# Forming the low part of each weight piece on GpSimd instead of VectorE

## The chip, the core and the metric

The kernel runs on one core of a Trainium2 chip. The metric is the device time of one execution in microseconds, the median over runs; a profile of one execution is beside it. The engines are TensorE (PE, matrix products; PEld is its loading of weights), VectorE (DVE), ScalarE (ACT), GpSimd (POOL) and SyncE (SP, which issues the DMAs). Each engine works through its own list of instructions in order, and waits at an instruction until the ones that it depends on have reported.

## The reference

```python
def _attn_ref(q, k, v):                       # 2 x 8 heads, 768 positions, 64 wide
    block, window = (32, 16)
    k_sum = k.reshape(B, H, nb, block, D).max(axis=3)
    v_sum = v.reshape(B, H, nb, block, D).mean(axis=3)
    scores_l = scale * np.matmul(q, k.transpose(0, 1, 3, 2))    # masked to |i - j| < window
    scores_s = scale * np.einsum('bhsd,bhnd->bhsn', q, k_sum) + np.log(block)
    a = softmax over both together
    return np.matmul(a, v_all)                # v and v_sum

x = attention output, 1536 tokens x 512
y = (x @ w_a) * (x @ w_b) @ w_out             # 512 -> 1536 -> 512
h = y @ w_in;  out = np.maximum(0.01 * h, h) @ w_out2   # 512 -> 2048 -> 512
```

q, k, v and the result are float32. The five dense weights arrive as float64, two 32-bit words for a number; the kernel builds a float32 value from both words.

## The kernel before

Attention is done in pairs of windows (transposes, scores, a softmax on ScalarE and VectorE, transposes of the weights, products with v), and writes x as two float32r tiles, a high part (rounded) and the low part that is left. Every dense product is then three matmuls: high by high, high by low, low by high (`mm3`, L580). One such matmul has 512 columns.

The weights come in 68 pieces of 128 x 512 numbers (`a` and `b`, f = 0 to 11; `o`, 12; `i` and `p`, 16 each). A piece is staged by a DMA of 512 KB and converted in seven steps: `low` (L337, VectorE, and L341, ScalarE), `clamp` (L345), `shift` (L350), `join` (L356), `add` (L362), all on VectorE, `high` (L367: ScalarE rounds to float32r) and `rest_of` (L370: the float32 value less that rounded part, the low part of the piece). The steps stand in a list, `bg`, from which a few are taken at a time between the products (`interleave`, `tick`). A piece lies in one of 14 early buffers, later of 8 more, until its last use. The tile `wc` has two buffers: a piece's L341 needs that the subtraction (L370) of the piece two before is done.

The dense part has nine passes, `units`: (s, c) with s a third of the hidden size (four f) and c one of three chunks of 512 tokens. A pass runs four pairs of an a product and a b product (12 matmuls each), and after each pair forms g = a * b and splits it: ScalarE copies a (L608), VectorE multiplies (L612), ScalarE rounds (L600), VectorE subtracts (L601, tile gs). Then the pass's y products run (48 matmuls in four groups of 12, two groups at a time: the first three f of both, 18 matmuls, then the fourth f of both). The last gs of a pass is therefore first read by the 19th matmul of its y products. While s = 0 the attention of the next chunk runs between the products. The last stage (L787, L788, L601) does the same for h, with the o products one product behind.

The order of each engine's list is made by the framework's scheduler when the program is built, from times that it assumes for each instruction; it need not be the order of the code. GpSimd has, after some constants at the start, one kind of work: the copies of the block sums of v into the windows (`put_sums`, L191), 16 of them, the last at about 140 us. Attention's other steps on VectorE that are named below are L528 (scores, reads PSUM), L542 (weights times 1/sum, reads SBUF), L479 and L428 (reductions), L573 (low part of x, one operand in PSUM); L680 and L685 gather y from PSUM.

Of the kernel before, what the change touches and what calls it, by code (L numbers as in the profile page):

```python
# [21 lines left out]
def kernel(  # L22
# [12 lines left out]
    nc = tc.nc  # L35
# [269 lines left out]
    def stage():  # L305
        key = pieces[cnt["st"]]
        cnt["st"] += 1
        nm, f = key
        t = wst_p.tile([P, 1024], I32, tag="wst", name="wst")
        if nm in "op":  # L310
            src = {"o": w_o, "p": w_o2}[nm][P * f : P * (f + 1), :]
            nc.sync.dma_start(out=t, in_=src)
        else:
            src = {"a": w_a, "b": w_b, "i": w_i}[nm][:, 2 * P * f : 2 * P * (f + 1)]
            nc.sync.dma_start(
                out=t.rearrange("p (k f) -> p k f", k=KT),
                in_=src.rearrange("(k p) f -> p k f", p=P),
            )
        staged[key] = t

    def convert():

        i = cnt["conv"]
        key = pieces[i]
        while cnt["st"] < min(i + 4, len(pieces)):
            stage()
        cnt["conv"] += 1
        ww = staged.pop(key).rearrange("p (f two) -> p f two", two=2)
        lo_w, hi_w = ww[:, :, 0], ww[:, :, 1]
        home = "early" if room["early"] else "late"  # L330
        assert room[home], key
        room[home] -= 1
        t = {}

        def low():
            t["r"] = wcv_p.tile([P, 512], I32, tag="wr", name="wr", bufs=1)
            nc.vector.tensor_scalar(  # L337
                out=t["r"], in0=lo_w.bitcast(U32), scalar1=2.0**-29, scalar2=None, op0=ALU.mult
            )
            t["c"] = wcv_p.tile([P, 512], I32, tag="wc", name="wc")  # L340
            nc.scalar.activation(out=t["c"].bitcast(F32), in_=hi_w.bitcast(F32), func=AF.Abs)  # L341

        def clamp():
            c = t["c"].bitcast(F32)
            nc.vector.tensor_scalar(  # L345
                out=c, in0=c, scalar1=F_LO, scalar2=F_HI, op0=ALU.max, op1=ALU.min
            )

        def shift():
            nc.vector.tensor_scalar(  # L350
                out=t["c"], in0=t["c"], scalar1=3, scalar2=0x3FFFFFF8,
                op0=ALU.logical_shift_left, op1=ALU.bitwise_and,
            )

        def join():
            nc.vector.scalar_tensor_tensor(  # L356
                out=t["c"], in0=hi_w, scalar=-0x40000000, in1=t["c"],
                op0=ALU.bitwise_and, op1=ALU.bitwise_or,
            )

        def add():
            nc.vector.tensor_tensor(out=t["c"], in0=t["c"], in1=t["r"], op=ALU.add)  # L362

        def high():
            pool = wsp_p if home == "early" else late["wsp"]
            t["w"] = pool.tile([P, 2, 512], F32R, tag="wsp", name="wsp")
            nc.scalar.copy(out=t["w"][:, 0], in_=t["c"].bitcast(F32))  # L367

        def rest_of():
            nc.vector.tensor_tensor(  # L370
                out=t["w"][:, 1], in0=t["c"].bitcast(F32), in1=t["w"][:, 0].bitcast(F32),
                op=ALU.subtract,
            )
            w_of[key] = t["w"], home

        bg.extend([low, clamp, shift, join, add, high, rest_of])
# [454 lines left out]
```

## Time and profile before

| | us |
|---|---|
| median of 3 runs | 662.12 (661.54 to 662.96) |
| the profiled execution | 661.62 |
| its span, first to last instruction | 659.9 |
| TensorE busy | 635.6 |
| VectorE busy | 422.0 |
| ScalarE busy | 267.8 |
| GpSimd busy | 21.1 |

The span is that of one execution taken by the hardware profiler; 1.7 us of its time lie around it. Busy time is the time in which an engine has an instruction under way; matmuls overlap, and their ends are modelled. A wait is put down to the instruction that reported last before the waiting one began. The granted clock is the share of TensorE's full speed that the chip allowed in a stretch.

### The profile page before, as it was taken

The numbers are of one execution on the slowest core, as the hardware profiler recorded it, in microseconds if no ns is written. First come the engines' busy times: TensorE is split into PE (matmuls) and PEld (weight loads), VectorE is DVE, ScalarE is ACT, GpSimd is POOL, SyncE is SP. The second block draws the span as 40 slices with busy tenths as digits, with TensorE's granted clock in tenths as the row PEclk, the third lists the DMA queues.
The fourth block names the chain that finished last, engine by engine and source line by source line (L and its number), as shares of the span: only waits on it lengthen the run. The fifth ranks groups of instructions, "written<-read, shape, count | busy, mean of one in ns | idle before, by whom it ended". The sixth has DMA issues, their size and how long they took to land.

```text
span 659.9 us, 9321 instructions
## 1 busy us (share of the span) xinstructions
PE 635.6 (96%) x3448; PEld 518.4 (79%) x3448; DVE 422.0 (64%) x968; ACT 267.8 (41%) x607; POOL 21.1 (3%) x38
## 2 busy tenths in 40 slices
PE   5699799999999999999999999999999999999997
PEld 4567577777888888888888888888888888888886
DVE  5989999955999972699623779732279532422323
ACT  4677386653445421344222535322255322222221
POOL 3210020000000000000000000000000000000000
PEclk9899799999999999999999999999999999999999
DMA  9976543512334430143200232400014000100101
GB/s 239 258 174 162 148 107 109 151 26 65 125 130 133 156 96 1 64 125 121 74 1 0 67 93 77 147 1 1 0 51 141 1 0 1 64 1 1 64 1 64
DMA packets 72590, 53.43 MB, mean 81 GB/s; under 512 B 46176, under 2 KB 66656, under 8 KB 72544
## 3 DMA queue, kind: packets, MB, share of 16 engines
q1 hardware_dynamic: 72544, 52.84, 27.0%
q8 instruction: 27, 0.44, 0.3%
q14 instruction: 19, 0.16, 0.1%
HBM read 49.68 MB, written 3.15 MB: 80 GB/s over the span
## 4 chain that ended last, share of the span: by engine, by line
PE 89%; DVE 7%; ACT 2%; DMA 1%; issue 1%; SPq 0%; DVEq 0%; ACTq 0%
PE ps_t L580 38%; PE ps_c L580 19%; PE ps_a L580 14%; PE ps_b L580 13%; PE ps_t L515 2%; DVE pm L528 1%; PE ps_t L550 1%; PE ps_t L562 1%; ACT pm L532 1%; DVE v L428 1%; DVE pm L542 1%; DMA wst<-in_moe_w_b_dram 1%; DVE wc L356 1%; PE ps_t L497 1%; DVE wr L337 0%
## 5 line engine op out<-in xcount | busy, mean ns | idle before, releaser
L580 PE MATMUL ps_t<-x,wsp 128*128 128x512 f32 x336 | 78.6, 389 | 0.0
L580 PE MATMUL ps_c<-wsp,gs 128*128 128x512 f32 x288 | 75.8, 389 | 0.0
L580 PE MATMUL ps_t<-wsp,gs 128*128 128x512 f32 x288 | 74.7, 389 | 0.0
L580 PEld LDWEIGHTS ps_t<-x,wsp 128*128 128x128 f32 x336 | 63.1, 188 | 13.1
L580 PE MATMUL ps_t<-ys,wsp 128*128 128x512 f32 x288 | 71.9, 389 | 0.0
L580 PE MATMUL ps_a<-x,wsp 128*128 128x512 f32 x252 | 68.6, 410 | 3.0 <-DVE wsp L370 2.7
L341 ACT ACTIVATE wc<-wst 128x512 f32<-128x512 f32 x68 | 45.6, 673 | 55.3 <-DMA wst<-in_moe_w_out_dram 12.1
L580 PE MATMUL ps_b<-x,wsp 128*128 128x512 f32 x252 | 64.3, 394 | 0.5 <-DVE wsp L370 0.5
L580 PEld LDWEIGHTS ps_t<-ys,wsp 128*128 128x128 f32 x288 | 54.1, 188 | 11.2
L580 PEld LDWEIGHTS ps_c<-wsp,gs 128*128 128x128 f32 x288 | 54.0, 188 | 11.2
L580 PEld LDWEIGHTS ps_t<-wsp,gs 128*128 128x128 f32 x288 | 54.0, 188 | 11.2
L580 PE MATMUL ps_c<-gs,wsp 128*128 128x512 f32 x240 | 60.8, 394 | 0.0
L580 PEld LDWEIGHTS ps_a<-x,wsp 128*128 128x128 f32 x252 | 47.9, 194 | 14.2 <-DVE wsp L370 3.1
L788 DVE SCALAR_TENSOR_TENSOR h<-h,ps_t 128x512 f32<-128x512 f32 x24 | 16.5, 686 | 60.8 <-ACT h L787 60.8
L580 PEld LDWEIGHTS ps_b<-x,wsp 128*128 128x128 f32 x252 | 46.6, 188 | 10.6 <-DVE wsp L370 1.0
L370 DVE TENSOR_TENSOR wsp<-wc,wsp 128x512 fp32r<-128x512 f32 x68 | 47.2, 696 | 9.9 <-ACT wsp L367 9.8
L580 PEld LDWEIGHTS ps_c<-gs,wsp 128*128 128x128 f32 x240 | 44.4, 188 | 9.5 <-ACT x L572 0.2
L367 ACT CAST wsp<-wc 128x512 fp32r<-128x512 f32 x68 | 42.1, 622 | 19.6 <-DVE wc L362 13.8
L580 PE MATMUL ps_t<-gs,wsp 128*128 128x512 f32 x192 | 47.7, 390 | 0.0
L601 DVE TENSOR_TENSOR gs<-h,gs 128x512 fp32r<-128x512 f32 x48 | 33.1, 691 | 22.8 <-ACT gs L600 22.7
L362 DVE CUSTOM_DVE_ANT_0 wc<-wc,wr 128x1024 uint16<-128x1024 uint16 x68 | 46.6, 685 | 0.6
L356 DVE SCALAR_TENSOR_TENSOR wc<-wst,wc 128x512 int32<-128x512 int32 x68 | 46.7, 689 | 0.2
(86 smaller groups left out, 835.9 us busy)
## 6 DMA issues: line engine op xcount, KB each, us to landing
wst<-in_moe_w_out_dram SPq DMA_DIRECT2D x28, 512.0 KB, 3.3
wst<-in_moe_w_in_dram SPq DMA_DIRECT2D x16, 512.0 KB, 3.7
wst<-in_moe_w_a_dram SPq DMA_DIRECT2D x12, 512.0 KB, 3.6
wst<-in_moe_w_b_dram SPq DMA_DIRECT2D x12, 512.0 KB, 3.6
k<-in_k_dram SPq DMA_DIRECT2D x16, 192.0 KB, 3.5
vb<-in_v_dram SPq DMA_DIRECT2D x6, 512.0 KB, 5.3
out_dram<-acc SPq DMA_DIRECT2D x12, 256.0 KB, 2.1
q<-in_q_dram SPq DMA_DIRECT2D x16, 128.0 KB, 2.9
```

Source lines behind the costliest of these rows:

```text
L341: nc.scalar.activation(out=t["c"].bitcast(F32), in_=hi_w.bitcast(F32), func=AF.Abs)
L356: nc.vector.scalar_tensor_tensor(out=t["c"], in0=hi_w, scalar=-0x40000000, in1=t["c"], op0=ALU.bitwise_and, op1=ALU.bitwise_or,)
L362: nc.vector.tensor_tensor(out=t["c"], in0=t["c"], in1=t["r"], op=ALU.add)
L367: nc.scalar.copy(out=t["w"][:, 0], in_=t["c"].bitcast(F32))
L370: nc.vector.tensor_tensor(out=t["w"][:, 1], in0=t["c"].bitcast(F32), in1=t["w"][:, 0].bitcast(F32), op=ALU.subtract,)
L428: lambda i=i, d=d: nc.vector.tensor_reduce(out=v0[:, i, d : d + D // 2], in_=vb_tiles[i][:, :, d : d + D // 2].rearrange("p j d -> p d j") ...
L497: nc.tensor.transpose(ps[:, n * P : (n + 1) * P], q2[:, n].rearrange("p c d -> p (c d)"), ident)
L515: nc.tensor.matmul(out=ps[h, w, :], lhsT=qt[h, w * W : (w + 1) * W], rhs=kts[h, (g * G + w) * SC : (g * G + w) * SC + P], start=True, stop ...
L528: pace["after"] = nc.vector.tensor_tensor_reduce(out=pm[:, w, :], in0=ps[:, w, :], in1=m, scale=1.0, scalar=3.0e38, op0=ALU.add, op1=ALU.m ...
L580: nc.tensor.matmul(out=ps, lhsT=w(a), rhs=x(b), start=first and j == 0, stop=last and j == 2)
L601: nc.vector.tensor_tensor(out=t[:, 1], in0=src, in1=t[:, 0].bitcast(F32), op=ALU.subtract)
L788: nc.vector.scalar_tensor_tensor(out=h, in0=h, scalar=0.01, in1=ps, op0=ALU.mult, op1=ALU.max)
```

## The change

`rest_of` is issued on GpSimd instead of VectorE. Operands, types and tiles stay.

```diff
         def rest_of():
-            nc.vector.tensor_tensor(
+            nc.gpsimd.tensor_tensor(
                 out=t["w"][:, 1], in0=t["c"].bitcast(F32), in1=t["w"][:, 0].bitcast(F32),
                 op=ALU.subtract,
             )
```

The scheduler makes new lists from it. GpSimd, from its first copies on (vw_99 and vw_100 are the two tiles of windows of v; wsp is a piece's high and low part), before:

```order
L191 COPY vw_99<-vs 24x1024
L191 COPY vw_100<-vs 24x1024
L191 COPY vw_99<-vs 24x1024
L191 COPY vw_100<-vs 24x1024
L191 COPY vw_99<-vs 24x2x256 x2
L191 COPY vw_100<-vs 24x2x256 x2
L191 COPY vw_99<-vs 24x2x256 x2
```

And now:

```order
L191 COPY vw_99<-vs 24x1024
L191 COPY vw_100<-vs 24x1024
L191 COPY vw_99<-vs 24x1024
L370 TENSOR_TENSOR wsp<-wc,wsp 128x512 x2
L191 COPY vw_100<-vs 24x1024
L191 COPY vw_99<-vs 24x2x256 x2
L370 TENSOR_TENSOR wsp<-wc,wsp 128x512
L191 COPY vw_100<-vs 24x2x256
L370 TENSOR_TENSOR wsp<-wc,wsp 128x512
L191 COPY vw_100<-vs 24x2x256
L370 TENSOR_TENSOR wsp<-wc,wsp 128x512 x2
```

The subtractions stand between the copies; 14 come before the last copy, 54 behind it.

VectorE at the second piece, early in attention (wc and wr are the piece being converted, pm and nb the scores), before:

```order
L362 ISA wc<-wc,wr 128x1024
L542 TENSOR_TENSOR pm<-pm,sm 128x512
L486 COPY kts_94<-ks_98 128x12x24
L370 TENSOR_TENSOR wsp<-wc,wsp 128x512
L528 ISA pm,nb<-ps_t_509,negm_first 128x128
```

And now:

```order
L362 ISA wc<-wc,wr 128x1024
L542 TENSOR_TENSOR pm<-pm,sm 128x512
L486 COPY kts_94<-ks_98 128x12x24
L528 ISA pm,nb<-ps_t_509,negm_first 128x128
L528 ISA nb 128x1
```

L370 is gone from the list, and the scores follow directly.

VectorE at the end of the fourth pass (s = 1, c = 0), up to its last gs, before:

```order
L362 ISA wc<-wc,wr 128x1024
L345 TENSOR_SCALAR wc<-wc 128x512
L337 TENSOR_SCALAR wr<-wst 128x512
L350 TENSOR_SCALAR wc<-wc 128x512
L370 TENSOR_TENSOR wsp<-wc,wsp 128x512
L356 SCALAR_TENSOR_TENSOR wc<-wst,wc 128x512
L612 TENSOR_TENSOR g<-ps_t_2614,g 128x512
L362 ISA wc<-wc,wr 128x1024
L345 TENSOR_SCALAR wc<-wc 128x512
L337 TENSOR_SCALAR wr<-wst 128x512
L601 TENSOR_TENSOR gs<-g,gs 128x512
```

And now:

```order
L350 TENSOR_SCALAR wc<-wc 128x512
L356 SCALAR_TENSOR_TENSOR wc<-wst,wc 128x512
L362 ISA wc<-wc,wr 128x1024
L345 TENSOR_SCALAR wc<-wc 128x512
L337 TENSOR_SCALAR wr<-wst 128x512
L350 TENSOR_SCALAR wc<-wc 128x512
L612 TENSOR_TENSOR g<-ps_t_2614,g 128x512
L356 SCALAR_TENSOR_TENSOR wc<-wst,wc 128x512
L362 ISA wc<-wc,wr 128x1024
L601 TENSOR_TENSOR gs<-g,gs 128x512
```

More conversion steps stand in front of the same L612 and L601. From the last L601 of the third pass to this one the list held nine L362, eight L356 and eight L370 before; now it holds ten L362 and ten L356.

## Rows read from the trace of the kernel before

**Rows 1.** The page: busy us and share of each engine; VectorE in 40 slices.
```profile
PE 635.6 (96%) x3448; PEld 518.4 (79%) x3448; DVE 422.0 (64%) x968; ACT 267.8 (41%) x607; POOL 21.1 (3%) x38
...
DVE  5989999955999972699623779732279532422323
```

**Rows 2.** Windows: start:end us, length, busy of each engine, granted clock, DMA.
```profile
16.50:99.00 82.50, 69.37 (x707) 54.11 (x708) 76.78 (x251) 57.45 (x195) 11.76 (x13) 0.94 0.65 170
...
69.20:75.80 6.60, 5.06 (x16) 3.67 (x18) 6.60 (x12) 1.07 (x2) 0.00 (x0) 0.50 0.73 197
99.00:165.00 66.00, 66.00 (x508) 50.43 (x507) 48.16 (x154) 37.23 (x109) 4.08 (x3) 1.00 0.30 88
165.00:231.00 66.00, 66.00 (x293) 54.62 (x292) 62.61 (x126) 31.97 (x54) 0.00 (x0) 1.00 0.41 136
```

**Rows 3.** Waits: engine, what waited <- for what: total us, times, longest.
```profile
PE ps_a L580 <- DVE wsp L370: 2.7, 1, 2.7
...
PE ps_t L562 <- POOL vw L191: 1.0, 1, 1.0
...
ACT wc L341 <- DMA wst<-in_moe_w_out_dram: 12.1, 8, 2.3
```

**Rows 4.** Groups by line, and L191 alone: duration ns min/median/max.
```profile
L370 DVE TENSOR_TENSOR wsp<-wc,wsp 128x512 fp32r<-128x512 f32 x68 | 47.2, 696 | 9.9 <-ACT wsp L367 9.8
...
L191 POOL COPY vw<-vs x16: 607/1081/1507, 20.5 to 140.0; 24x1024 f32<-24x1024 f32 x8, 24x512 f32<-24x512 f32 x8
```

**Rows 5.** Windows of L370 alone: start:end, length, VectorE busy.
```profile
16.50:99.00 82.50, 6.26 (x8) 0.94 0.65 170
```

**Rows 6.** Timeline of VectorE beside two copies: start us, duration us, instruction.
```profile
105.13 0.69 DVE L362 CUSTOM_DVE_ANT_0 wc<-wc,wr 128x1024 uint16<-128x1024 uint16 x1
105.74 1.26 DVE L345 TENSOR_SCALAR wc<-wc 128x512 f32<-128x512 f32 x1
...
123.87 0.69 DVE L573 TENSOR_TENSOR x<-ps_t,x 128x512 fp32r<-128x512 f32 x1
124.48 0.61 DVE L350 TENSOR_SCALAR wc<-wc 128x512 int32<-128x512 int32 x1
```

**Rows 7.** Timeline of GpSimd: copies of 1024 elements; the first meets no wait.
```profile
94.39 1.10 POOL L191 COPY vw<-vs 24x1024 f32<-24x1024 f32 x1 [6.36 <-PE ps_t L562]
105.32 1.40 POOL L191 COPY vw<-vs 24x1024 f32<-24x1024 f32 x1 [9.84 <-PE ps_t L562]
123.35 1.46 POOL L191 COPY vw<-vs 24x1024 f32<-24x1024 f32 x1 [16.64 <-PE ps_t L562]
```

**Rows 8.** Timeline of VectorE at the end of the third pass.
```profile
189.60 0.42 DVE L350 TENSOR_SCALAR wc<-wc 128x512 int32<-128x512 int32 x1
189.94 0.68 DVE L370 TENSOR_TENSOR wsp<-wc,wsp 128x512 fp32r<-128x512 f32 x1
190.54 0.68 DVE L356 SCALAR_TENSOR_TENSOR wc<-wst,wc 128x512 int32<-128x512 int32 x1
191.14 0.68 DVE L601 TENSOR_TENSOR gs<-g,gs 128x512 fp32r<-128x512 f32 x1
191.74 0.68 DVE L362 CUSTOM_DVE_ANT_0 wc<-wc,wr 128x1024 uint16<-128x1024 uint16 x1
```

**Rows 9.** The fourth pass: its last L601, and the chain with its y products.
```profile
222.87 0.69 DVE L601 TENSOR_TENSOR gs<-g,gs 128x512 fp32r<-128x512 f32 x1
...
220.96 4.08 PE ps_c L580 x18
225.04 2.04 PE ps_t L580 x9
```

**Rows 10.** Timeline at the longest early wait: a rounding, its subtraction, the product.
```profile
63.50 0.62 ACT L367 CAST wsp<-wc 128x512 fp32r<-128x512 f32 x1
...
70.01 0.68 DVE L370 TENSOR_TENSOR wsp<-wc,wsp 128x512 fp32r<-128x512 f32 x1
...
70.74 1.65 PE L580 MATMUL ps_a<-x,wsp 128*128 128x512 f32 x3 [2.71 <-DVE wsp L370]
```

## The prediction

> **What bounds the kernel now.** I read the page first. TensorE is busy for 635.6 of 659.9 us and VectorE for 422.0 [rows 1], so by the averages VectorE has room; the windows by stage say when that is false. From 99 us to the tail TensorE has no idle time at all; nearly all that it loses lies ahead: 13.1 us of idle between 16.5 and 99 us, with VectorE busy for 76.78 of those 82.5 us, and a granted clock of 0.94 there [rows 2]. Half of full speed (1.2 instead of 2.4 GHz) was granted from 69.2 to 75.8 us, right behind TensorE's longest stall in that part, and cost 3.3 us of work; the other 0.06 x 82.5 - 3.3 = 1.7 us is a shorter dip [rows 2]. Between 165 and 231 us VectorE is nearly full again, 62.61 of 66 us, but TensorE runs through [rows 2]. So two stages can answer: the first 99 us, where freed VectorE time could become TensorE time, and the full stretch behind 165 us, where a slower VectorE could stop TensorE. Third, the list of TensorE's waits: the one for the moved line (L370) is 2.7 us, once [rows 3]. Fourth, the groups and single instructions of L370 and of GpSimd's only steady work, the copies of L191 [rows 4 to 7].
>
> **What the change removes.** 68 subtractions leave VectorE, 47.2 us by their durations [rows 4]. Instructions there overlap a little: start to start such a one takes 0.60 us (189.94, 190.54, 191.14, 191.74), a one-operand conversion step 0.34 (189.60 to 189.94) [rows 8]. I use 0.60 for each two-operand step ("heavy") and 0.335 for L337, L345 and L350 ("light"). So a piece costs VectorE 2 x 0.60 + 3 x 0.335 = 2.2 us instead of 2.8.
>
> **What it adds.** The trace shows no GpSimd subtraction, but GpSimd copies beside VectorE, and they exclude each other. The copy that starts at 105.32 finds L362 (two SBUF operands) running until 105.82 and ends only at 106.72; L345, next on VectorE, takes 1.26 us instead of 0.42 and ends at 107.00, just behind it [rows 6, 7]. At 123.35 the copy again waits for L362; L573, which has one operand in PSUM, runs beside it in its usual 0.69, and L350 behind that waits for the copy's end [rows 6, 7]. So a GpSimd instruction that reads SBUF holds something that all of L337, L345, L350, L356, L362, L601 and L542 want (the steps that read SBUF alone, many elements at a time), whoever waits gets it next, and steps that read PSUM pass. The hold of a 1024-element copy is 106.72 - 105.82 = 0.90 us; one without a wait lasts 1.10, so 0.20 lies outside the hold [rows 7].
>
> How long does a 512-element subtraction hold? From below: the shortest copy of 512 elements takes 0.607 [rows 4], less 0.20 is 0.41, were the second operand free. From above: two such copies one after the other, 1.21. The subtraction reads 2 x 512 elements, as many as the 1024-element copy, and so that row is nearest: I take 0.90. The GPSIMD Engine Reference of the Trainium skill (section 3.1, elementwise cycle accounting) says that the two reads of one instruction take turns on one port and puts a two-input op at about 2.6 cycles an element; by that 512 elements are about 1.1 us, an estimate, and no run here shows it yet. With it the sum would come out as in the second rival.
>
> The table of VectorE's order shows what stands behind each subtraction now. ScalarE's rounding (L367) takes 0.62 [rows 10], so with the hand-overs GpSimd is ready about 0.8 us behind each L362: two light steps or one heavy one later. What comes then on VectorE decides whether the hold is paid.
>
> *Until 99 us.* Eight subtractions leave VectorE, 6.26 us busy [rows 5]: 8 x 0.61 plus two waits for copies of some 0.5, say 5.8. Of the first eight pieces four (first, third, fourth, fifth) have SBUF work behind them: 4 x 0.90; the other four have a run of eight L528, which read PSUM, and cost at most 0.1 each. Together 4.0, so VectorE wins 1.8 us. The next six pieces, until about 132 us, win 6 x 0.61 = 3.7 and pay about 6 x 0.75 = 4.5, since nearly all have SBUF work behind them: minus 0.8. The stage comes out about 1 us shorter. There is a second, loose gain: at 70.01 the subtraction stood behind reductions, though its rounding had ended at 64.12, and TensorE waited 2.71 us for it [rows 10]; an empty GpSimd queue would have it done near 65.4. But VectorE stays full, and TensorE then waits for the next thing that VectorE makes. I count 1.0 us in all; ends: 5 us gained (wait and clock dip both gone, hold 0.41), 3 us lost (hold 1.21). GpSimd's own queue holds back little: the order puts the subtractions between the copies about where L370 stood in time; TensorE's one wait for a copy is 1.0 now [rows 3].
>
> *The fourth pass (s=1, c=0), about 192 to 225 us.* Its y products need the last gs (L601) at their 19th matmul: that one starts at 225.04, and L601 ends at 222.87 + 0.69 = 223.56 [rows 9]. So there are 1.5 us to spare. The new order has, from the last L601 of the third pass to that of the fourth, 30 light and 30 heavy steps (10 each of L337, L345, L350, L356, L362, four L612, four L601, two L680): 10 full pieces, where before there were 8 L370, 26 light and 27 other heavy. Work: 30 x 0.335 + 30 x 0.60 = 28.05 us. From 191.74, when the third pass's L601 makes way [rows 8], to 225.04 are 33.3. That leaves 5.2 us for ten holds; they come to 10 x 0.90 = 9.0, of which some 1.3 lie beside L612 and L680 (PSUM). VectorE is late by 28.05 + 9.0 - 1.3 - 33.3 = 2.5 us, and TensorE, in order, stands at the 19th matmul for it. By the same sum before: 35 x 0.60 + 26 x 0.335 = 29.7, which fits. Breakeven is a hold of (5.2 + 1.3) / 10 = 0.65. The stall is followed by a clock dip or it isn't; 1.7 to 3.3 us by the two dips above; I count 1.5.
>
> *All else from 132 us.* By the order passes five and eight have no conversion between their last steps, and the others fewer pieces than the fourth (the third 7, the sixth 4, the ninth 5). In the last stage hs is wanted a whole product of 12 matmuls later, 2.7 us by the 4.08 for 18 [rows 9], which hides a hold. Nothing counted; in the ninth pass up to 0.9, where the hold is over 1.0.
>
> **Sum.** Profiled execution: 661.62 us, which is 0.5 under the median of the three runs (662.12). 661.6 - 1.0 + 2.5 + 1.5 = 664.6, and with that 0.5: 665.1 us.
>
> **Rivals.** *Faster.* The hold is near 0.41 to 0.5, or the holds fall into VectorE's pauses. Then a piece costs VectorE 2.2 + 0.45, less than 2.8; the fourth pass is on time (28.05 + 4.5 < 33.3), and the early stage wins up to 5 us: 662.1 - 4.5 = 657.6. For: one-input copies of 512 elements take only 0.607 [rows 4]; early VectorE is the limit [rows 2]. Against: two operands must be read. It decides from a hold under 0.65.
>
> *Slower by more.* The subtraction holds longer than the copy, 1.1 (between 0.90 and 1.21): the fourth pass is late by 28.05 + 11 - 1.3 - 33.3 = 4.5, passes three and nine by some 1.2 together, the early stage loses 1, the clock dip is full (3.3) with half a chance for a second: 661.6 + 4.5 + 1.2 + 1 + 2.5 = 670.8, to the median 671.3. For: arithmetic on GpSimd can't be cheaper than a copy. Against: no row prices it.
>
> *No change.* Hold about 0.65, or the fourth pass isn't as dense on the chip as in the order, since pieces also wait for their DMA; the early win and the late loss cancel: 662. For: ScalarE's L341 waits 12.1 us for one weight's DMAs alone [rows 3], so conversion isn't paced by VectorE alone. Against: VectorE's 62.61 of 66 us [rows 2].
>
> **Chances.** Forecast 0.42, slower by more 0.18, no change 0.20, faster 0.20. Three runs of this kernel differ by 0.2%, so within 660.8 to 663.4 is no change: faster 0.20, same 0.20, slower 0.60. The range leaves a tenth on either side: half of the faster case below, and holds near 1.21 above (28.05 + 12.1 - 1.3 - 33.3 = 5.6, plus two dips and 3 early, some 675): 658.5 to 672. The likeliest case alone: 663.5 to 667.5.
>
> **What would show it.** L370 on GpSimd with a mean of 1.1 to 1.4 us (0.90, 0.20 and waits); mean times of L345, L337, L350 and L356 up by some 0.1 to 0.25 each, L528 and L612 unchanged; a new wait of TensorE for DVE gs L601 near 225 us, some 2.5 us long; the granted clock behind it at half for some microseconds, or not; idle time before 99 us a little under 13.1. Wrong: L370 near 0.65 us and no wait for gs; or TensorE waiting for wsp L370 by GpSimd, which would mean that its queue, not the hold, is the price.

## The result and the profile after

The changed kernel takes 671.59 us (median of 4 runs, 670.54 to 673.03), the kernel before 661.83 in the same comparison: ratio 1.0146, 95% interval 1.0123 to 1.017. It is slower, by 9.8 us; a loss of 3 us was forecast. The profiled execution took 671.36 us with a span of 669.3.

The page of the changed kernel, busy time by engine, and the group of the moved line (columns as in [rows 1, 4]):

```profile
PE 641.4 (96%) x3448; PEld 520.2 (78%) x3448; DVE 435.4 (65%) x900; ACT 268.6 (40%) x607; POOL 117.9 (18%) x106
...
L370 POOL TENSOR_TENSOR wsp<-wc,wsp 128x512 fp32r<-128x512 f32 x68 | 96.5, 1422 | 351.7 <-ACT wsp L367 339.2
...
L356 DVE SCALAR_TENSOR_TENSOR wc<-wst,wc 128x512 int32<-128x512 int32 x68 | 60.2, 885 | 1.3
...
L362 DVE CUSTOM_DVE_ANT_0 wc<-wc,wr 128x1024 uint16<-128x1024 uint16 x68 | 51.8, 762 | 1.0
```

VectorE lost 68 instructions and 47.2 us of work [rows 4], and its busy time rose from 422.0 [rows 1] to 435.4 us: an instruction that is held counts as busy, so the wait for GpSimd stands in the durations of others (L356 had a mean of 689 ns before, L362 685). No group of waits names it; it has to be read from means that grew.

The windows (columns as in [rows 2]):

```profile
16.50:99.00 82.50, 69.76 (x708) 53.09 (x710) 79.20 (x252) 58.78 (x200) 23.02 (x21) 0.97 0.66 172
99.00:165.00 66.00, 66.00 (x496) 50.09 (x496) 46.32 (x136) 34.25 (x102) 12.71 (x9) 0.99 0.29 85
165.00:231.00 66.00, 61.65 (x275) 49.85 (x272) 61.21 (x96) 31.43 (x53) 23.18 (x17) 0.99 0.37 120
```

TensorE had no idle time between 165 and 231 us; now it has 4.35 us. Its waits, beside [rows 3]:

```profile
PE ps_t L550 <- DVE pm L542: 5.5, 5, 1.9
PE ps_t L469 <- DMA k<-in_k_dram: 4.5, 1, 4.5
PE ps_c L580 <- ACT gs L600: 3.2, 1, 3.2
...
PE ps_a L580 <- ACT wsp L367: 0.9, 1, 0.9
```

The new wait is for gs, not for GpSimd's product, and it is not where the prediction put it. The timeline of TensorE at the y products of the fourth pass:

```profile
221.74 3.02 PE L580 MATMUL ps_t<-x,wsp 128*128 128x512 f32 x12 [0.68 <-DVE g L612]
224.60 1.52 PE L580 MATMUL ps_c<-gs,wsp 128*128 128x512 f32 x6
229.30 0.73 PE L580 MATMUL ps_c<-gs,wsp 128*128 128x512 f32 x2 [3.18 <-ACT gs L600]
230.52 3.95 PE L580 MATMUL ps_c<-gs,wsp 128*128 128x512 f32 x10 [0.49 <-DVE gs L601]
```

And VectorE, ScalarE and GpSimd in front of it:

```profile
226.06 1.39 POOL L370 TENSOR_TENSOR wsp<-wc,wsp 128x512 fp32r<-128x512 f32 x1 [3.28 <-ACT wsp L367]
226.36 1.63 DVE L356 SCALAR_TENSOR_TENSOR wc<-wst,wc 128x512 int32<-128x512 int32 x1
227.92 0.68 DVE L612 TENSOR_TENSOR g<-ps_b,g 128x512 f32<-128x512 f32 x1
228.63 0.62 ACT L600 CAST gs<-g 128x512 fp32r<-128x512 f32 x1 [0.21 <-DVE g L612]
```

TensorE stops at the seventh y matmul, and what it wants there is the rounded g of the third pair: L612 of this pass runs at 214.59, 221.00, 227.92 and 234.26 us, and the third is the one that the waiting matmul follows. The fourth pair's gs is read later and is not waited for.

The granted clock of the same place (columns: stretch, length, PE busy, clock, DMA share, GB/s):

```profile
226.10:229.30 3.20, 0.02 (x1) 1.00 0.43 126
229.30:229.80 0.50, 0.50 (x2) 1.00 0.73 238
229.80:233.20 3.40, 2.91 (x7) 0.55 0.27 102
233.20:234.30 1.10, 1.10 (x5) 0.85 0.56 209
```

Some 0.8 us after the stall ends the clock goes to its lower level (1.2 of 2.4 GHz), from 230.1 to 233.5 us: 3.4 us, spread over the last two of these stretches.

Where the 9.4 us of span lie is read from the start of each pass's first y product:

| first y product of pass | before, us | after, us | later by |
|---|---|---|---|
| 2 | 152.98 | 155.55 | 2.56 |
| 3 | 188.16 | 190.72 | 2.56 |
| 4 | 220.80 | 224.60 | 3.80 |
| 5 | 253.44 | 262.88 | 9.44 |
| 9 | 384.00 | 393.44 | 9.44 |

Two places, then: 2.56 us ahead of the second pass, 6.88 around the fourth, nothing anywhere else. Of the 6.88 us, 4.35 are TensorE's idle time, and the lower clock costs some 1.7 (half of 3.4); the 0.8 that remain are not accounted for.

### The profile page after: what moved, and what is told of

Its sections match the earlier page's. It is cut to its first block, busy times and chain, and to the rows that moved or that the text cites. A ratio compares the mean times of both kernels' runs of the same rounds, so it can differ in the third digit from the quotient of the medians.

```text
span 669.3 us, 9371 instructions
## 1 busy us (share of the span) xinstructions
PE 641.4 (96%) x3448; PEld 520.2 (78%) x3448; DVE 435.4 (65%) x900; ACT 268.6 (40%) x607; POOL 117.9 (18%) x106
## 4 chain that ended last, share of the span: by engine, by line
PE 82%; DVE 14%; issue 2%; ACT 1%; DMA 0%; POOL 0%; SPq 0%; ACTq 0%; DVEq 0%
PE ps_t L580 33%; PE ps_c L580 18%; PE ps_a L580 12%; PE ps_b L580 12%; PE ps_t L515 3%; DVE wc L356 2%; DVE wr L337 2%; PE ps_t L562 2%; DVE wc L350 1%; PE ps_t L550 1%; DVE v L428 1%; DVE wc L345 1%; DVE wc L362 1%; DVE pm L542 1%; DVE pm L528 1%
## 5 line engine op out<-in xcount | busy, mean ns | idle before, releaser
L370 POOL TENSOR_TENSOR wsp<-wc,wsp 128x512 fp32r<-128x512 f32 x68 | 96.5, 1422 | 351.7 <-ACT wsp L367 339.2
L341 ACT ACTIVATE wc<-wst 128x512 f32<-128x512 f32 x68 | 45.8, 674 | 60.1 <-POOL wsp L370 22.9
L580 PE MATMUL ps_c<-gs,wsp 128*128 128x512 f32 x240 | 62.6, 400 | 3.7 <-ACT gs L600 3.2
L356 DVE SCALAR_TENSOR_TENSOR wc<-wst,wc 128x512 int32<-128x512 int32 x68 | 60.2, 885 | 1.3
L362 DVE CUSTOM_DVE_ANT_0 wc<-wc,wr 128x1024 uint16<-128x1024 uint16 x68 | 51.8, 762 | 1.0
L601 DVE TENSOR_TENSOR gs<-h,gs 128x512 fp32r<-128x512 f32 x48 | 33.5, 698 | 24.7 <-ACT gs L600 24.7
```

The costliest lines, as they stand in the source:

```text
L356: nc.vector.scalar_tensor_tensor(out=t["c"], in0=hi_w, scalar=-0x40000000, in1=t["c"], op0=ALU.bitwise_and, op1=ALU.bitwise_or,)
L370: nc.gpsimd.tensor_tensor(out=t["w"][:, 1], in0=t["c"].bitcast(F32), in1=t["w"][:, 0].bitcast(F32), op=ALU.subtract,)
L580: nc.tensor.matmul(out=ps, lhsT=w(a), rhs=x(b), start=first and j == 0, stop=last and j == 2)
L601: nc.vector.tensor_tensor(out=t[:, 1], in0=src, in1=t[:, 0].bitcast(F32), op=ALU.subtract)
```

## The experiments

The columns "pass 2" and "pass 5" give how much later than before the first y product of that pass starts in the trace; their difference is what the fourth pass costs. Each ratio is to the kernel before in the same comparison, whose median lay between 661.80 and 662.70 us. Line numbers shift by a few where an edit adds or removes lines.

| kernel | us | ratio (95%) | pass 2 | pass 5 |
|---|---|---|---|---|
| the change | 671.59 | 1.0146 (1.0123 to 1.017) | +2.56 | +9.44 |
| e_early | 664.32 | 1.0025 (1.0011 to 1.004) | +1.93 | +1.93 |
| e_late | 669.34 | 1.0104 (1.0084 to 1.0125) | +0.47 | +7.59 |
| e_not4 | 664.63 | 1.0038 (1.0023 to 1.0053) | +2.84 | +2.84 |
| e_copy | 659.11 | 0.9948 (0.9929 to 0.9967) | -3.61 | -3.61 |
| e_copyhi | 662.72 | 1.0003 (0.9992 to 1.0014) | +1.22 | +1.22 |
| e_bc | 667.28 | 1.0071 (1.0054 to 1.0088) | +2.26 | +7.74 |
| e_fillcopy | 666.84 | 1.0078 (1.0051 to 1.0105) | +1.05 | +3.66 |
| e_wc3 | 677.08 | 1.0225 (1.0205 to 1.0245) | +2.91 | +11.89 |
| e_half | 661.39 | 0.9988 (0.9973 to 1.0003) | -1.58 | -0.22 |
| e_half14 | 660.58 | 0.9976 (0.9967 to 0.9986) | -0.34 | -0.34 |
| e_sel | 667.94 | 1.0087 (1.0071 to 1.0104) | +6.95 | +6.95 |

### The two places apart: e_early, e_late, e_not4

The same line in three kernels, with another condition in each (`i` is a piece's number of 68; the late ones are converted from the third pass on):

```diff
-            nc.vector.tensor_tensor(
+            e = nc.gpsimd if i < 14 else nc.vector            # e_early
+            e = nc.gpsimd if i >= 14 else nc.vector           # e_late
+            e = nc.gpsimd if not 18 <= i < 34 else nc.vector  # e_not4
+            e.tensor_tensor(
```

**e_early.** 

> GpSimd subtracts for the first 14 pieces alone, VectorE for the other 54; VectorE's list from the third pass on is that of the kernel before. Hold (mine): the changed kernel was 2.56 us behind at the start of the third pass, so 661.8 + 2.6 = 664.4 us (663.4 to 665.5), no wait of TensorE for gs in the fourth pass, L337, L345, L350 and L356 back at 0.42 to 0.69 us behind 165 us. Rival, the order (more pieces packed ahead of the fourth pass's last gs): nothing on the early part, so 662 if the early 2.56 us are luck of the schedule elsewhere, 664 if not.

**e_late.** 

> VectorE subtracts for the first 14 pieces, GpSimd for the other 54; VectorE's list in passes three and four is that of the changed kernel (7 and 10 pieces). Hold: the changed kernel lost 9.44 - 2.56 = 6.9 us behind the start of the third pass, so 661.8 + 6.9 = 668.7 us (667 to 670), with a wait for gs of some 3 to 4 us in the fourth pass and a clock dip behind it. If it is below 664, the late loss needs the early one, and I am wrong on where it comes from.

**e_not4.** 

> GpSimd subtracts for 52 of the 68 pieces; the 16 with numbers 18 to 33, converted in passes three to five, stay on VectorE. Hold where VectorE is full: the fourth pass is on time, the early loss stays, pass seven and nine pay nothing: 661.8 + 2.6 = 664.4 us (663 to 666). Rival, a price for each subtraction moved (9.8 us / 68 = 0.14 us each): 661.8 + 7.5 = 669 us.

All three came out as expected. With the first 14 subtractions on GpSimd the program loses 1.9 us early and nothing later; with the other 54 it has the whole loss of the fourth pass (7.12), with the same wait:

```profile
PE ps_c L581 <- ACT gs L601: 3.2, 1, 3.2
```

With 52 on GpSimd, but none of those that are converted around the fourth pass, that loss is gone. So it isn't the number of moved subtractions that costs: 34 of them, behind the fourth pass, cost nothing that can be seen.

### What a GpSimd instruction holds: e_copy, e_copyhi, e_bc

One instruction on GpSimd in each, of the same size, at the same point of the code:

```diff
-            nc.vector.tensor_tensor(
-                out=t["w"][:, 1], in0=t["c"].bitcast(F32), in1=t["w"][:, 0].bitcast(F32),
-                op=ALU.subtract,
-            )
+            nc.gpsimd.tensor_copy(out=t["w"][:, 1], in_=t["c"].bitcast(F32))          # e_copy
+            nc.gpsimd.tensor_copy(out=t["w"][:, 1], in_=t["w"][:, 0].bitcast(F32))    # e_copyhi
+            nc.gpsimd.tensor_tensor(                                                  # e_bc
+                out=t["w"][:, 1], in0=t["c"].bitcast(F32),
+                in1=t["w"][:, 0, 0:1].bitcast(F32).to_broadcast([P, 512]), op=ALU.subtract,
+            )
```

**e_copy.** 

> GpSimd copies the unrounded value into the low part instead of subtracting (one SBUF operand; the low part is not the reference's). VectorE's list has ten pieces in the fourth pass as in the changed kernel. Hold: a copy of 512 elements holds 0.45 us, under the 0.65 at which the fourth pass is just on time: no wait for gs there, and early VectorE gains: 657 to 661.5 us. Order (ten pieces ahead of the last gs, whatever GpSimd does): the late loss stays, 666 to 669 us. Latency of the GpSimd step (0.6 instead of 1.4 us until wc is free): as the hold, 657 to 662.

**e_copyhi.** 

> GpSimd copies the rounded high part into the place of the low part: one operand, but it waits for ScalarE's rounding as the subtraction does, which the copy of the unrounded value did not. The products use that copy as low part. The plain copy of 512 elements held for about 0.47 us and took 3.6 us off the time. Theory size of the hold: the dependency costs nothing by itself, the fourth pass has 28.05 + 4.7 of 33.3 us and stays on time, no wait of TensorE for a gs: 658.5 to 661. Rival dependency: GpSimd is ready only one or two steps behind each add, then takes the access in front of a light step, and the plain copy was cheap only because it started earlier; then the fourth pass is late again by 2 us or more, with a wait for gs, and the time is 664 to 668.

**e_bc.** 

> GpSimd subtracts, but its second operand is one element of the rounded high part, repeated over the row (the low part is then something else). Dependency and instruction kind are those of the changed kernel, and the lists of the engines are the nearest to it of all that I built. Theory two reads: the second operand's 512 reads are what lengthens the hold; if the repeated element is not read again, the hold is near the copy's 0.47 and the time 658.5 to 662 with no wait for gs; if it is read 512 times, the hold is 1.15 again and the time 670 to 673 with the fourth pass late by some 7 us. Rival, the order of the lists: the time is near 671 whatever the hold.

The hold can be read wherever GpSimd itself waits for a VectorE step and then runs: it is the time from the end of that step to GpSimd's own end. In the changed kernel:

```profile
229.79 0.68 DVE L601 TENSOR_TENSOR gs<-g,gs 128x512 fp32r<-128x512 f32 x1
229.93 1.67 POOL L370 TENSOR_TENSOR wsp<-wc,wsp 128x512 fp32r<-128x512 f32 x1 [2.48 <-ACT wsp L367]
230.39 1.49 DVE L350 TENSOR_SCALAR wc<-wc 128x512 int32<-128x512 int32 x1
```

L601 ends at 230.47, GpSimd at 231.60: 1.13 us, and L350, which takes 0.42 alone, ends 0.28 behind it. In e_bc and in e_copyhi:

```profile
222.60 0.69 DVE L601 TENSOR_TENSOR gs<-g,gs 128x512 fp32r<-128x512 f32 x1
222.66 1.52 POOL L370 TENSOR_TENSOR wsp<-wc,wsp 128x512 fp32r<-128x512 f32 x1 [2.05 <-ACT wsp L367]
```

```profile
216.78 0.68 DVE L598 TENSOR_TENSOR gs<-g,gs 128x512 fp32r<-128x512 f32 x1
216.83 1.11 POOL L370 CAST wsp<-wsp 128x512 fp32r<-128x512 f32 x1 [2.65 <-ACT wsp L367]
```

That is 0.89 and 0.48. Over all such pairs of a trace (30 to 40 of each kind, nearly all within 0.03 of the median) the medians are 1.149 us for the subtraction of two full operands, 0.899 with one element as second operand, and 0.473 for a copy. Some 0.12 to 0.14 lie outside the hold (shortest durations 1.270, 1.039 and 0.608).

In e_copy ten pieces stand in VectorE's list of the fourth pass, as in the change, and nothing is late: the order of that list alone is not the price there. The fourth pass goes by the hold: nothing lost at 0.473 (e_copy and e_copyhi), 5.48 at 0.899, 6.88 at 1.149; in the last two the clock falls for 3.4 us behind the stall. In e_bc the wait is there, somewhat shorter than the change's 3.18:

```profile
223.48 1.52 PE L580 MATMUL ps_c<-gs,wsp 128*128 128x512 f32 x6
227.78 4.86 PE L580 MATMUL ps_c<-gs,wsp 128*128 128x512 f32 x12 [2.77 <-ACT gs L600]
```

e_copyhi waits for ScalarE's rounding as the subtraction does, and its fourth pass is on time (18 y matmuls in a row, no wait): the rival that the dependency makes the pass late falls. e_bc came out between its two expectations, since its hold did. Its time settles something else: this hold is the 0.90 of the prediction, and the kernel with it is at 667.28, not 665.1. Its profiled execution (669.62) was the longest of its four (the others 666.44 to 667.58), with a granted clock of 0.92 in the window from 16.5 to 99 us, where the change had 0.97; so its early +2.26 is more than its median bears out.

e_copyhi missed its 658.5 to 661 by its early part, which lost 1.2 us where e_copy had gained 3.6, at the same hold.

### Any GpSimd access, or the sum of holds: e_fillcopy

Two one-operand instructions on GpSimd instead of one:

```diff
-            nc.vector.tensor_tensor(
-                out=t["w"][:, 1], in0=t["c"].bitcast(F32), in1=t["w"][:, 0].bitcast(F32),
-                op=ALU.subtract,
-            )
+            nc.gpsimd.memset(t["w"][:, 1].bitcast(F32), 0.0)
+            nc.gpsimd.tensor_copy(out=t["w"][:, 1], in_=t["c"].bitcast(F32))
```

> GpSimd fills the low part (writes only) and then copies the unrounded value into it (the low part is not the reference's): two instructions, together about as long as the subtraction (0.5 + 0.6 + a hand-over, 1.2 to 1.4 us until wc is free), of which only the copy reads SBUF. Hold by reads: 0.45 us a piece, no wait for gs in the fourth pass, 658 to 662 us. Hold by any SBUF use: 0.45 + 0.45, the fourth pass late by some 2 to 3 us, 663 to 667 us. Latency: as the changed kernel, 668 to 672 us, with L341 waiting for the copy as it now waits for L370 (22.9 us in total).

GpSimd and VectorE at the end of a piece in the fourth pass:

```profile
209.43 0.80 POOL L371 CAST wsp<-wc 128x512 fp32r<-128x512 f32 x1 [2.58 <-DVE wc L362]
210.17 0.52 POOL L370 MEMSET wsp<- 128x512 f32 x1
```

```profile
209.33 0.43 DVE L337 TENSOR_SCALAR wr<-wst 128x512 int32<-128x512 uint32 x1
209.67 1.30 DVE L345 TENSOR_SCALAR wc<-wc 128x512 f32<-128x512 f32 x1
```

L345 stands through both: the copy ends at 210.23, the memset at 210.69, L345 at 210.97, 0.28 behind it as L350 was behind the subtraction. A memset that only writes therefore holds such a one-operand step as well. Where the memset itself waited for one (14 times), the time from the end of that step to its own was 0.465 us. The two-operand steps it doesn't hold; they run beside it, both at their usual length:

```profile
495.65 0.69 DVE L362 CUSTOM_DVE_ANT_0 wc<-wc,wr 128x1024 uint16<-128x1024 uint16 x1
495.84 0.53 POOL L370 MEMSET wsp<- 128x512 f32 x1 [3.25 <-PE ps_t L578]
```

The mean of L362 and L356 is 689 and 688 ns in this kernel, 685 and 689 before, while L337 grew from 450 to 684 and L350 from 422 to 504. The kernel's time, 666.84, is in the range named for a hold by any access to SBUF (663 to 667), and the fourth pass lost 2.6 us. The sum of the two holds doesn't give that loss: 0.473 + 0.465 is more than e_bc's 0.899, and e_bc lost 5.48. Two things differ: the memset lets the two-operand steps pass, and no fall of the clock follows here. How much each is worth was not separated. The expectation by latency falls: the two last nearly as long as the subtraction (583 and 746 ns on average, against 1422) and cost far less; the time lies below the 668 to 672 that latency asked for.

### Latency instead of hold: e_wc3

The subtraction also ends later than VectorE's did, and ScalarE's L341, which needs the piece two before to be done, waits 22.9 us for GpSimd in the changed kernel. With a third buffer it needs the piece three before:

```diff
-            t["c"] = wcv_p.tile([P, 512], I32, tag="wc", name="wc")
+            t["c"] = wcv_p.tile([P, 512], I32, tag="wc", name="wc", bufs=3)
```

> The changed kernel with three wc buffers instead of two, so that a piece's L341 no longer waits for the subtraction of the piece two before it. VectorE's list still has ten pieces in the fourth pass. Hold (each subtraction on GpSimd holds 1.15 us, as the waits of the changed kernel show): no better, 668 to 674 us, with a wait for gs in the fourth pass. Rival, latency (wc comes free 0.7 us later, which slows conversion): most of the loss is gone, 662 to 666 us.

```profile
PE ps_c L580 <- ACT gs L600: 4.6, 3, 3.3
...
PE ps_a L580 <- ACT x L572: 2.2, 2, 1.8
PE ps_c L580 <- DVE gs L601: 2.0, 3, 0.9
```

677.08 us: worse than the change by 5.5, and out of the expected range on the far side. The edit took away less of the wait than it was meant to; L341's wait for GpSimd over the whole program, in the change and then with three buffers:

```profile
ACT wc L341 <- POOL wsp L370: 22.9, 22, 1.6
```

```profile
ACT wc L341 <- POOL wsp L370: 17.9, 17, 1.5
```

So the run alone doesn't settle latency. The trace of the changed kernel does, for the fourth pass: from 196.5 to 230 us L341 waits for DMAs alone and never for GpSimd, and VectorE, where the steps follow, is busy for 30.25 of the 30.80 us up to the late L612 (197.12 to 227.92). It isn't short of input there; it is held. Why three buffers made it worse was not separated; more pieces were begun ahead of the fourth pass's last gs (11 L345 instead of 10), and TensorE waited for gs and x in more places.

### Half of the columns: e_half, e_half14

```diff
-            nc.vector.tensor_tensor(
-                out=t["w"][:, 1], in0=t["c"].bitcast(F32), in1=t["w"][:, 0].bitcast(F32),
-                op=ALU.subtract,
-            )
+            c, hi = t["c"].bitcast(F32), t["w"][:, 0].bitcast(F32)
+            halves = ((nc.gpsimd, slice(0, 256)), (nc.vector, slice(256, 512)))
+            for e, h in halves if i < 14 else ((nc.vector, slice(0, 512)),):    # e_half: halves for every i
+                e.tensor_tensor(
+                    out=t["w"][:, 1, h], in0=c[:, h], in1=hi[:, h], op=ALU.subtract
+                )
```

**e_half.** 

> GpSimd subtracts columns 0 to 255 of each piece, VectorE columns 256 to 511. Hold in proportion to the columns: 0.55 to 0.6 us a piece, and a half step of about 0.34 on VectorE; in the fourth pass 29 x 0.60 + 29 x 0.335 + 9 x 0.34 + 10 x 0.59 - 0.7 - 33.3 = 2.0 us late, with half a clock dip 3 to 4, early 0 to 1.5 us lost: 664 to 668 us. If the hold were a fixed price of each GpSimd instruction (1.15 us whatever its size), VectorE would have more to do than in the changed kernel: 672 to 678 us.

**e_half14.** 

> Columns 0 to 255 of the low part on GpSimd and 256 to 511 on VectorE for the first 14 pieces only; the other 54 wholly on VectorE as before. With all 68 pieces split the first three passes came out 1.6 us earlier and the fourth 1.4 later. Theory, the two stages add up and are independent: 1.6 us earlier from the second pass on and nothing lost later, 660.2 us, ratio 0.9976. Rival: the gain ahead of the second pass was one of the scheduler's list and not of the split, and another list gives it back: 661.8 or more.

e_half missed its 664 to 668 on the fast side: the fourth pass lost only 1.36 us, 0.64 of it as a wait for gs. The hold of 256 columns, read as above, is 0.598 us, so it isn't a fixed price of each instruction. e_half14, the split kept to the first 14 pieces, hit its number: 660.58 us, 0.24% faster than before (0.14 to 0.33), and the one version with the reference's result that is faster than both kernels by more than its interval. In its trace the early gain is 0.34 us and not the expected 1.6, so the number was hit with less than the mechanism promised; its profiled execution (661.34) was longer than its median. The trace doesn't show the split as the source of that gain; it speaks for the rival, the scheduler's list (see the early stage, below).

### Which early pieces: e_sel

```diff
-            nc.vector.tensor_tensor(
+            e = nc.gpsimd if i in (1, 5, 6, 7) else nc.vector
+            e.tensor_tensor(
```

> GpSimd subtracts for four pieces of the attention stage alone, the second, sixth, seventh and eighth; all others stay on VectorE. In this kernel's list the second and the eighth have runs of L528 (reads PSUM) where the hold falls, the sixth half a run, the seventh small steps and reductions. Hold: four steps of 0.6 us leave VectorE and about 1.5 us of holds are paid, so up to 1 us gained: 660.5 to 662.5 us, a version that may beat both. If a GpSimd subtraction cost VectorE its whole 1.15 us wherever it falls, 2.2 us lost: 664.

A miss, by 5.4 us beyond the range. The four pieces were chosen for the PSUM work or the small steps behind them, where a hold costs little. But the new condition gave the scheduler other lists, and VectorE's had this:

```profile
68.20 3.03 DVE L429 TENSOR_REDUCE v<-vb 128x32 f32<-128x512 f32 x3
71.15 0.68 DVE L602 TENSOR_TENSOR gs<-g,gs 128x512 fp32r<-128x512 f32 x1
71.75 2.84 DVE L429 TENSOR_REDUCE v<-vb 128x32 f32<-128x512 f32 x3
74.50 0.68 DVE L362 CUSTOM_DVE_ANT_0 wc<-wc,wr 128x1024 uint16<-128x1024 uint16 x1
```

```profile
75.89 1.22 PE L581 MATMUL ps_b<-x,wsp 128*128 128x512 f32 x2 [4.78 <-ACT wsp L367]
```

Six reductions of a later window stand in front of a piece's last VectorE step, and TensorE waits 4.78 us for that piece. No GpSimd instruction is in it. Yet this wait isn't the 6.95 us. Up to the second pass's first y product TensorE is busy for 139.95 us:

```profile
0.00:159.93 159.93, 139.95 (x1204) 107.58 (x1205) 129.20 (x436) 98.53 (x324) 26.20 (x42) 0.96 0.54 144
```

That leaves 19.98 us of idle time, no more than before (20.50); what grew is the time of the matmuls, by 7.5 us. The lower clock has a part in it (13.7 us at the lower level up to there, against 10.2 before), and the order of TensorE's list a larger one, as follows.

### The early stage, read again

In the early stage neither hold nor count orders the kernels (+2.56, +1.93, +1.22, -3.61, -0.34). What TensorE did up to the first y product of the second pass, with the same 1204 matmuls ahead of it, in before, after and e_half14 (columns of [rows 2]; x1205 where the stretch just takes in the y product):

```profile
0.00:152.98 152.98, 132.48 (x1204) 102.68 (x1205) 129.61 (x440) 98.89 (x324) 21.08 (x38) 0.97 0.57 150
```

```profile
0.00:155.55 155.55, 135.71 (x1205) 103.70 (x1206) 132.09 (x426) 99.33 (x324) 40.95 (x52) 0.98 0.56 148
```

```profile
0.00:152.64 152.64, 132.03 (x1204) 102.97 (x1205) 129.39 (x439) 99.16 (x324) 33.14 (x52) 0.98 0.57 150
```

Idle time is 20.50 us before (152.98 - 132.48), 19.84 after, 20.61 in e_half14; e_early has 19.35, e_copyhi 19.57. The change made TensorE's early idle time shorter by 0.66. What grew is the time of the matmuls, by 3.23, though the clock was no worse. By form, before and then after, to 153 us:

```profile
L515 PE MATMUL ps_t<-kts,qt 64*64 64x128 f32 x384 | 28.5, 286 | 2.8 <-DVE ks L479 1.6 <-DVE kts L486 0.9 <-ACT pt L552 0.2
...
L562 PE MATMUL ps_t<-pt,vw 128*64 128x64 f32 x352 | 14.3, 227 | 1.5 <-POOL vw L191 1.0 <-ACT pt L552 0.4
```

```profile
L515 PE MATMUL ps_t<-kts,qt 64*64 64x128 f32 x384 | 30.5, 292 | 2.7 <-DVE ks L479 1.3 <-DVE kts L486 0.9 <-ACT pt L552 0.3
...
L562 PE MATMUL ps_t<-pt,vw 128*64 128x64 f32 x352 | 15.8, 227 | 1.4 <-POOL vw L191 1.0 <-ACT pt L552 0.4
```

The same 352 matmuls L562 have the same mean, and cover 1.5 us more: they overlap less. By their start times the change's list goes from an L562 to another line 21 times, before 15 times, and the start-to-start time at such a place is about 0.16 us, inside a run about 0.03.

The lines differ in the part of TensorE's array that a matmul uses, its tile, whose shape stands in the rows behind the names: 64*64 for L515, 128*64 for L562, 128*128 for most others. Take all places up to that y product where one matmul's tile has another shape than the next one's, and add up the time from start to start, idle time left out:

| kernel | places | us at them | idle us | first y product of pass 2 |
|---|---|---|---|---|
| before | 81 | 19.12 | 20.50 | |
| the change | 94 | 22.13 | 19.84 | +2.56 |
| e_early | 94 | 22.24 | 19.35 | +1.93 |
| e_late | 81 | 19.47 | 19.81 | +0.47 |
| e_copy | 89 | 20.84 | 16.30 | -3.61 |
| e_copyhi | 97 | 22.75 | 19.57 | +1.22 |
| e_half14 | 77 | 18.14 | 20.61 | -0.34 |
| e_sel | 97 | 23.99 | 19.98 | +6.95 |

A place takes 0.23 to 0.25 us on average in each of these traces. So 3.01 of the change's 3.23 us stand at 13 more such places: the early loss stands in TensorE's list, in which the scheduler put the attention's and the dense products in another order, and not in waits for VectorE. The gain of e_half14 (four places fewer) and most of the 7.5 us of e_sel (4.87) read the same way; e_copy is early by its idle time alone. This is read from the traces. No run changed that order alone, so that it is the cause of the early loss is likely and not shown.

## Why the prediction was wrong

**Sign of the whole, and the place of the late loss: right.** VectorE's relief was given back by GpSimd's hold, the fourth pass was the place where that reached TensorE, a fall of the clock followed, and passes from the fifth on lost nothing.

**"The subtraction reads 2 x 512 elements, as many as the 1024-element copy ... I take 0.90": mis-sized.** The hold is 1.149 us, near the upper end of what I had bounded (1.21). The row it was taken from is a one-operand instruction; a second operand cost more than as many elements of the first: 0.473 for a copy of 512, 1.149 for two operands of 512. With 1.149 the prediction's own sum for the fourth pass is 28.05 + 11.5 - 1.3 - 33.3 = 4.9 late, with the fall of the clock 6.4; measured 6.88. That is the second rival, and its 671.3 comes within 0.3 of the result partly by luck: it had 1.2 us for the third and the ninth pass, which lost nothing, and 1 us for the early stage, which lost 2.56. The GPSIMD Engine Reference of the Trainium skill (section 3.1) had the number that the copies didn't give: 2.6 cycles an element for two inputs, from which the prediction worked out about 1.1 us as an estimate. This case's trace agrees (1.149), and the Trainium skill's price for the very operation would have been the better choice over a row of another operation.

**"Its y products need the last gs (L601) at their 19th matmul": wrong, and not by chance harmless.** The stop is at the seventh matmul, for the third pair's gs. From the third pass's last L601 (its successor starts at 197.12) to that L612 VectorE's list has 24 light and 21 heavy steps: 24 x 0.335 + 21 x 0.60 = 20.6 us, and eight subtractions, 9.2 at 1.149: 227.0, seen 227.92. For no stop L612 had to start by 226.12 - 1.38 = 224.74 (1.38 from its start to the waiting matmul at 229.30), 3.18 earlier, which is 0.40 for each of the eight holds: break-even near 0.75, an estimate, and 0.87 if the step times of the sum are taken as they are; the prediction had 0.65. It agrees with the ladder, 0.473 on time and 0.899 late; in e_bc VectorE also stood twice for ScalarE there (0.42 us each). That the forecast's 2.5 us at a hold of 0.90 and e_bc's 2.77 are close is luck: the errors (another gs, two subtractions fewer) went against each other.

**"I count 1.0 us in all" for the early stage: wrong in sign.** Idle time fell by 0.66 us, as the list of signs at the prediction's end said it would, and the wait for L370 with the fall of the clock behind it, the loose gain, is gone; but waits for VectorE's pm (L542) rose from 2.9 to 5.5 us, and the stage got 2.56 longer. I had counted VectorE's time alone and taken TensorE's own work as fixed. It isn't: the scheduler made another list for it too, with 94 changes of tile shape instead of 81 and 3.01 us more at them. This term is the larger part of the error: 3.6 of 6.4 us (-1.0 forecast against +2.56), the fourth pass 2.9 (4.0 against 6.88).

**"I count 1.5" for the clock dip: near.** 3.4 us at the lower level cost about 1.7 (half of 3.4).

**The list of signs.** L370's mean was 1422 ns, just above the 1.1 to 1.4 named; L350 and L356 rose by 0.2 (422 to 619, 689 to 885 ns), L337 by 0.15, L345 by 0.06; L528 and L612, which read PSUM, stayed. TensorE waited nowhere for GpSimd's product.

## What to carry to other kernels

Work that goes from VectorE to GpSimd takes VectorE's time with it when both work in SBUF: price it by the hold of that very operation (here 1.149 us against the 0.60 that the step took on VectorE), not by its engine's idle time, and not by a copy. Find the first consumer on the waiting engine's own list; the code's order names another. And where a scheduler makes the lists, a change on one engine is a new order on all: compare the busy time of the same instructions, and the number of places where TensorE's list changes its tile shape, not the idle time alone, before a gain or a loss is put down to the edit.

## What the runs showed of the hardware

- GpSimd's hold of VectorE's SBUF steps, for 128x512 float32: copy 0.473 us, subtraction with one repeated element 0.899, with two full operands 1.149; for 128x256 with two operands 0.598. The repeated element costs 0.25 less than a full operand and 0.43 more than the copy.
- A GpSimd memset, which reads nothing, also holds VectorE's one-operand SBUF steps, for 0.465 us (L345 lasted 1.30 us through a copy and a memset); two-operand steps ran beside it at their usual 0.69.
- A change of tile shape between two matmuls took 0.23 to 0.25 us from start to start on average in each trace of the table above (77 to 97 places each); within a run of L562 (128x64) one started about every 0.03 us. So TensorE's busy time for the same matmuls moved by 3 us with their order.
- Executions of one kernel differed by up to 4.3 us (e_fillcopy, 665.35 to 669.62). In e_bc the longest, 669.62 us, had the lowest mean granted clock (0.987), the shortest, 666.44, the highest (0.995).
